# Half of batch 1's query turns by DMA, later loads of the query remainders, and one stored keys-by-values product for each batch, in a fused attention and expert layer

## The chip, the cores and the metric

One core of a Trainium2 chip. Times are device microseconds of that core, the median over runs in which the kernel before and the changed one alternate on the same chip. Profile times count from the start of the profiled span, which is some 1.8 us shorter than the timed run.

## The reference, cut to what matters

```python
def _attn_ref(q, k, v):                       # (8, 8, 576, 64) each
    q_s = softmax over the 64 channels of q   # cut: written out with max, exp, sum
    k_s = softmax over the 576 tokens of k
    kv  = einsum('bhsd,bhse->bhde', k_s, v)
    return einsum('bhsd,bhde->bhse', q_s, kv)

def _moe_ref(x, w_in, w_out, beta):           # x (4608, 512), d_ff = 2048
    h = x @ w_in
    return (h * sigmoid(beta * h)) @ w_out
```

Each batch's eight heads give 576 rows of x. The kernel treats 512 rows of each batch as a slab (slabs 0 to 7); the remaining 64 rows of all batches, the query remainders, form slab 8.

## The kernel before: the parts concerned

A slab has two passes on TensorE: pass 1 (x @ w_in, 64 matmuls of 128x512, ScalarE applies the activation), pass 2 (@ w_out, 64 more). The attention of the next batch is woven into pass 2 at given matmul counts. The queries must be turned (tokens to columns) for it: batch 1's on TensorE with a copy by ScalarE, later batches' by a transposing DMA. All loads go through SP's queue, in program order. Heads come in four pairs; QT holds turned queries, KVC the product of keys and values, XT the attention output in bf16.

```python
# batch 1's loads, in the stream that fills the first 45 us
load_wout(0); load_wout(4)
load_swapped(1, (0, 2, 3))      # query slots
load_wout(8)
load_swapped(1, (1,))
load_k(1, 4, (0, 1)); load_wout(12, 2); load_v(1, 4, (0, 1))
load_wout(14, 1); load_wout(15, 1)
for hp in (2, 3):
    load_k(1, 4, (hp,)); load_v(1, 4, (hp,))   # batch 1's last keys, last values

# slab 0, between its passes; then what is woven into pass 2 (counts from 65)
load(2)
scale_wout(0); scale_wout(4)                   # VectorE, w_out / beta
exp_q(1, (0, 1, 3, 2))                         # ScalarE
norm_main(1, 0, 1, POOL); norm_main(1, 1, 1, POOL); norm_main(1, 3, 1, POOL)
scale_wout(8)
norm_main(1, 2, 1, POOL)
todo = [(104, turn pairs 0, 1 on TensorE), (104.1, cast_v(1, 0) on ScalarE),
        (111, turn pairs 2, 3 on TensorE),
        (111.1, scale_wout(14, 2), exp_kc(1, 2), exp_kc(1, 3)),
        (116, kv_half(1, (7, 0), 0)),          # keys x values, pairs 0, 1
        (122, out_half(1, (1, 2), 0)), ...]    # outputs of pairs 0, 1 -> XT
# slab 1 starts
at(0, 0, 3)                                    # 3 matmuls of pass 1
kv_half(1, (7, 0), 2)                          # "second-half products": pairs 2, 3
at(1, 0, 3); at(0, 3, 5)
out_half(1, (7, 7, 7, 0), 2)                   # needs QT of pairs 2, 3
```

(The four lines of `todo` are paraphrased, the rest is cut.) The remainders of batches 0 to 3 are 16 small loads issued after batch 3's loads; the products of a remainder pair run in slabs 2, 3, 4 and 6.

The softmax here doesn't subtract the row's maximum and nothing guards it: scores larger than these inputs give would overflow.

Of the kernel before, what the change touches and what calls it, by code (L numbers as in the profile page):

```python
# [6 lines left out]
BF16 = mybir.dt.bfloat16  # L7
# [4 lines left out]
B = 8  # L12
# [151 lines left out]
def bass_efficient_attn_shen__then__act_swish_beta_kernel(  # L164
# [12 lines left out]
    with ExitStack() as es:  # L177
        def sb(name, shape, dt):
            return es.enter_context(nc.sbuf_tensor(name, shape, dt))
# [15 lines left out]
        VB = [sb(f"VB{i}", [128, NHP, NG, VW], BF16) for i in range(2)]  # L195
        QT = [sb(f"QT{i}", [128, NHP, SM], BF16) for i in range(2)]
        QTR = sb("QTR", [128, NHP, 128], BF16)
        KVC = [sb(f"KVC{i}", [128, NHP, D], BF16) for i in range(4)]
        RC = [sb(f"RC{i}", [128, NHP], F32) for i in range(2)]
        XT = [sb(f"XT{i}", [128, NM, SM], BF16) for i in range(2)]  # L200
        XT8 = sb("XT8", [128, NM, SM], BF16)
# [81 lines left out]
        def load(b):  # L283
            load_swapped(b)
            load_k(b)
            load_v(b)
            if b % 2:
                load_qrem(b - 1)


        for hp in range(NHP):
# [118 lines left out]
        def tile_mm(bk, ro, co, c, w, l, r_, start, stop, r):  # L410
            mm(PS[bk][co:co + 64, c:c + w], l, r_, start, stop, r=r, w=[("ps", bk)], bk=bk,
               tp=(ro, co))

        def kvc(b):
            return b + 2 if b < 2 else b % 2

        def quad(hp):
            return ((hp, 0, 0), (hp, 64, 64), (hp + 1, 0, 64), (hp + 1, 64, 0))
# [68 lines left out]
            out_evac(b, bks, (a, a + 1))  # L487

        def block(b):
            rem = {3: 3, 4: 1, 5: 5, 7: 7}.get(b)  # L490
            if b + 1 < B:
                kv_prods(b + 1, (1, 2), (0, 2))
            out_prods(b, (5, 6, 7, 0))
            if rem:
                outr_prods(rem, (1, 2))
            out_evac(b, (5, 6, 7, 0))
            if rem:
                outr_evac(rem, (1, 2))
            if b + 1 < B:
                kv_evac(b + 1, (1, 2))  # L500
# [16 lines left out]
        def kv_tiles(hp, bk):  # L517
            for j in range(NG):
                for c in (0, 64):
                    p = slice(c, c + 64)  # L520
                    tile_mm(bk, c, 64 - c if hp % 2 else c, 0, D + 1, EK[0][p, hp, j, :],
                            VB[0][p, hp, j, 0:D + 1], j == 0, j == NG - 1,
                            [("ekc", 0, hp), ("vb", 0, hp, 0), ("vb", 0, hp, 1), ("vone", 0)])
            add(DVE, lambda e: e.reciprocal(RC[0][:, hp:hp + 1], PS[bk][:, D:D + 1]),
                r=[("ps", bk)], w=[("rc", 0, hp)], bank=[bk])
            o, p_ = KVC[2][:, hp, :], PS[bk][:, 0:D]
            v_ = bass.AP(RC[0], hp, [[NHP, 128], [0, D]])
            add(DVE, lambda e: e.tensor_tensor(o, p_, v_, ALU.mult), r=[("ps", bk), ("rc", 0, hp)],
                w=[("kvc", 2, hp)], bank=[bk])

        def out_now(b, hp, bk, eng):
            i = b % 2
            for c in (0, 64):
                p = slice(c, c + 64)
                tile_mm(bk, c, 64 - c if hp % 2 else c, 0, SM, KVC[2][p, hp, :], QT[0][p, hp, :], True, True,
                        [("kvc", 2, hp), ("qt", 0, hp)])
            add(eng, lambda e: (e.copy if eng == ACTE else e.tensor_copy)(
                XT[i][:, hp, :], PS[bk][:, :]),
                r=[("ps", bk)], w=[("xt", i, hp)], bank=[bk])

        def go(steps):
            for s in steps:
                s()
# [143 lines left out]
                at(m)  # L687
        load_wout(0)
        load_wout(4)
        load_swapped(1, (0, 2, 3))  # L690
        load_wout(8)
        load_swapped(1, (1,))
        load_k(1, 4, (0, 1))
        load_wout(12, 2)
        load_v(1, 4, (0, 1))
# [51 lines left out]
        for t in range(NSLAB):  # L747
            todo = []
            if t == 0:
                def evacs():  # L750
                    o2_evac(0, 0, 3, DVE)
                    o2_evac(0, 1, 4, ACTE)

                todo = [(104, lambda: go(t_steps(1, (0, 1), (1,), ACTE))),
                        (104.1, lambda: cast_v(1, 0, ACTE)),
                        (111, lambda: go(t_steps(1, (2, 3), (2,), ACTE))),
                        (111.1, lambda: (scale_wout(14, 2), exp_kc(1, 2), exp_kc(1, 3))),
                        (116, lambda: kv_half(1, (7, 0), 0)),
                        (122, lambda: out_half(1, (1, 2), 0)), (124.5, evacs)]
            elif t == 1:  # L760
                todo = [(103, lambda: (kv_prods(2, (1, 2), (0, 2)), kv_evac(2, (1, 2)))),
                        (118, lambda: block(2))]
            elif t < 7:
                todo = [(104, lambda: block(t + 1))]
            todo = sorted(todo, key=lambda x: -x[0])
            slot = [0]

            def tick():
                slot[0] += 1
                while todo and todo[-1][0] <= slot[0]:  # L770
                    todo.pop()[1]()

            if 2 <= t < 7:
                if t < 5:
                    load(t + 2 if t == 2 else t + 3)
                for hp in (0, 2):
                    norm_main(t + 1, hp, 2)
                    t_dma(t + 1, hp, 2)
                if t in (2, 3, 4, 6):
                    norm_rem(t // 2 if t != 3 else 0)  # L780
                    tr_dma(t // 2 if t != 3 else 0)
                if t == 2:
                    load(5)
            elif t == 1:
                for hp in range(NHP):
                    cast_v(2, hp)
            if t < 2:
                slot[0] = NM * FIRST[t]
            for f in range(FIRST[t] if t < 2 else 0, NF):
                pass1_tile(t, f, tick)  # L790
            if t == 0:
                load(2)
                scale_wout(0)
                scale_wout(4)
                exp_q(1, (0, 1, 3, 2))
                norm_main(1, 0, 1, POOL)
                norm_main(1, 1, 1, POOL)
                norm_main(1, 3, 1, POOL)
                scale_wout(8)
                norm_main(1, 2, 1, POOL)  # L800
                exp_kc(1, 0, 2)
                scale_wout(12, 2)
                for hp in range(1, NHP):
                    cast_v(1, hp)
                pass2_group(0, (0, 1, 2, 3), (3, 4, 5, 6), tick)
                while todo:
                    todo.pop()[1]()
                at = by_m(1, 0, FIRST[1])
                o2_evac(0, 2, 5, ACTE)
                o2_evac(0, 3, 6, DVE)  # L810
                add(ACTE, lambda e: e.activation(DUMMY[:, 2:3], WARM[:, 0:1], ACT.Silu),
                    r=["warm"], w=["dummy"])
                at(0, 0, 3)
                kv_half(1, (7, 0), 2)
                at(1, 0, 3)
                at(0, 3, 5)
                out_half(1, (7, 7, 7, 0), 2)
                at(0, 5)
                at(1, 3)
                at(2)  # L820
                at(3)
                store(0)
                load(3)
                load_qrem(0)
                continue
            nb = [t + 2] if t + 2 < B else []
            if t == 1:
                nb = [2, 3]
            late = []
            for b in nb:  # L830
                if t == 1 and b == 2:
                    exp_q(2)
                    for hp in range(2):
                        norm_main(2, hp, 1, POOL)
                    t_dma(2, 0, 2)
                for hp in (0, 2):
                    exp_kc(b, hp, 2)
                if b > 2:
                    late.append(b)
                if b > 3:  # L840
                    for hp in range(NHP):
                        cast_v(b, hp)
            for b in late:
                exp_q(b)
                if b % 2 == 1:
                    exp_qr(b // 2)
                if b == 3:
                    exp_qr(0)
            for u in range(4):
                if (t, u) == (8, 3):  # L850
                    last_tile(u, ((0, 384), (384, 512)), (OB[orot[0] % 2], MB[0]))
                    continue
                pass2_group(t, (u,), (OB[orot[0] % 2],), tick)
                orot[0] += 1
                if t == 1 and u == 0:
                    for hp in range(2, 4):
                        norm_main(2, hp, 1, POOL if hp == 2 else DVE)
                    t_dma(2, 2, 2)
                    for hp in range(NHP):
                        cast_v(3, hp)  # L860
            while todo:
                todo.pop()[1]()
            if t < 8:
                store(t)
# [30 lines left out]
```

## Time and profile before

| | before |
|---|---|
| time, median of 3 (range) | 279.93 us (279.82 to 280.27) |
| span of the profile | 278.7 us |
| TensorE busy | 97% |
| stream of loads | 375 to 402 GB/s from 7 to 56 us |
| pass 2 of slab 0, first matmul to slab 1's first | 28.66 to 44.91 us |
| second-half products of batch 1 start | 45.68 us |

In a timeline line the columns are start, length, engine, source line, operation, output<-inputs, shapes, count; the bracket gives the idle time before the group and what ended it. PEld lines are TensorE's weight loads. In the trace of before, every change from 128x128 to 64x64 tiles shows 0.42 us of idle in the weight loads, whatever it is labelled, so only longer idle, or idle at another place, is read as a wait here. The prediction below shows the lines.

### The profile page before, as it was taken

The page shows a single profiled execution, that of the slowest core. Times are in us where ns is not written, and L with a number is a line of the kernel's source. Part 1 is how long each engine was busy: PE and PEld are TensorE (multiplying, and loading weights), DVE is VectorE, ACT ScalarE, POOL GpSimd, SP SyncE. Part 2 cuts the span into 40 slices and gives each one's busy share as a digit, 9 for nine tenths or more (in the row PEclk, how much of TensorE's full clock was granted, in tenths as well). Part 3 has the DMA queues.
Part 4 walks back from the last instruction along what each step waited for, and adds up shares of the span by engine and source line. Part 5 has one row for each costly group of instructions (what it writes and reads, how often), then busy time and mean ns, then how long its engine had stood idle before and what let it go on. Part 6 is the DMA issues. An engine that isn't in the chain of part 4 may idle for free.

```text
span 278.7 us, 4595 instructions
## 1 busy us (share of the span) xinstructions
PE 270.9 (97%) x1899; PEld 131.2 (47%) x1929; DVE 103.0 (37%) x204; ACT 166.5 (60%) x240; POOL 34.9 (13%) x52
## 2 busy tenths in 40 slices
PE   7999999999999999999999999999999999999995
PEld 3544444444445454545454544444444444444443
DVE  4744786008590149205730462035603300110012
ACT  4767667799577736793579437853751175027500
POOL 2630241207000304030002000000000000000000
PEclk9999999999999999999999999999999999999999
DMA  7999999996489799960599133002600120011022
GB/s 235 385 384 402 388 390 375 399 361 112 45 287 371 200 317 304 389 133 2 152 383 212 30 150 75 2 4 94 151 0 2 56 94 2 0 75 75 2 71 79
DMA packets 42173, 50.12 MB, mean 180 GB/s; under 512 B 21028, under 2 KB 29476, under 8 KB 41000
## 3 DMA queue, kind: packets, MB, share of 16 engines
q1 hardware_dynamic: 41312, 48.90, 55.3%
q10 hardware_dynamic: 840, 0.93, 1.0%
q8 instruction: 15, 0.25, 0.4%
q14 instruction: 6, 0.05, 0.0%
HBM read 36.71 MB, written 9.44 MB: 166 GB/s over the span
## 4 chain that ended last, share of the span: by engine, by line
PE 83%; DMA 11%; SPq 3%; issue 1%; DVE 0%
PE PS L372 83%; DMA O2S<-in_moe_w_out_dram 4%; DMA WST<-in_moe_w_out_dram 4%; DMA WST<-in_moe_w_in_dram 3%; SPq L250 1%; SPq L569 1%; SPq L293 0%; DVE WOUT L562 0%; SPq L298 0%; DVE WIN L573 0%; DVE O2S L724 0%; SPq L147 0%
## 5 line engine op out<-in xcount | busy, mean ns | idle before, releaser
L648 ACT ACTIVATE GT<-PS,BETA 128x512 bf16<-128x512 f32 x144 | 96.4, 690 | 61.9 <-PE PS L372 61.8
L372 PE MATMUL PS<-WOUT,GT 128*128 128x512 bf16 (+2 forms) x574 | 125.7, 373 | 2.0 <-issue 1.1
L372 PE MATMUL PS<-XT,WIN 128*128 128x512 bf16 x565 | 125.8, 379 | 0.9 <-issue 0.3
L372 PEld LDWEIGHTS PS<-XT,WIN 128*128 128x128 bf16 x576 | 60.2, 106 | 64.0 <-issue 1.0
L372 PEld LDWEIGHTS PS<-WOUT,GT 128*128 128x128 bf16 x592 | 56.4, 98 | 66.5 <-DVE WOUT L562 1.2
L703 DVE COPY O2S<-PS 128x512 f32<-128x512 f32 x33 | 22.7, 688 | 124.4 <-PE PS L372 124.3
L357 POOL CAST VB<-VF 128x576 bf16<-128x576 f32 x29 | 20.5, 707 | 85.4 <-DMA VF<-in_v_dram 84.2
L338 DVE TENSOR_REDUCE QS<-EQ 128x8 f32<-128x512 bf16 (+1 forms) x22 | 20.1, 913 | 17.6 <-ACT EQ L314 17.6
L459 ACT CAST XT<-PS 128x512 bf16<-128x512 f32 x14 | 7.6, 587 | 23.0 <-PE PS L372 22.8
L322 ACT ACTIVATE EK<-KF 128x1152 bf16<-128x1152 f32 (+1 forms) x19 | 18.4, 1005 | 4.1 <-DMA KF<-in_k_dram 3.9
L314 ACT ACTIVATE EQ<-QF 128x512 bf16<-128x512 f32 x32 | 17.7, 616 | 3.8 <-DMA QF<-in_q_dram 3.7
L340 DVE TENSOR_TENSOR EQ<-EQ,QI 128x1024 bf16<-128x1024 bf16 (+1 forms) x12 | 14.4, 1200 | 0.4
L340 POOL TENSOR_TENSOR EQ<-EQ,QI 128x512 bf16<-128x512 bf16 x10 | 10.5, 1048 | 31.5 <-DVE QI L339 31.2
L459 DVE CAST XT<-PS 128x512 bf16<-128x512 f32 x14 | 9.1, 687 | 12.7 <-PE PS L372 12.7
L372 PEld LDWEIGHTS PS<-VB,EK 64*64 64x64 bf16 x576 | 6.6, 107 | 4.5 <-issue 2.5
L372 PE MATMUL PS<-VB,EK 64*64 64x65 bf16 x576 | 7.9, 193 | 0.4 <-POOL VB L357 0.3
L372 PE MATMUL PS<-XT 128*128 128x512 f32 x6 | 5.3, 1050 | 1.5 <-DVE XT L226 1.5
L648 ACT ACT_TABLE_LOAD x5 | 6.4, 1283 | 0.1
L372 PE MATMUL PS<-QT,KVC 64*64 64x512 bf16 x64 | 6.2, 383 | 0.1
L562 DVE TENSOR_SCALAR WOUT<-O2S,RB 128x512 bf16<-128x512 f32 x8 | 5.2, 686 | 1.0 <-DMA O2S<-in_moe_w_out_dram 0.9
L339 DVE RECIPROCAL QI<-QS 128x8 f32<-128x8 f32 (+1 forms) x22 | 5.0, 226 | 0.8
L322 ACT ACT_TABLE_LOAD x4 | 5.1, 1283 | 0.1
(51 smaller groups left out, 68.0 us busy)
## 6 DMA issues: line engine op xcount, KB each, us to landing
out_dram<-O2S SPq DMA_DIRECT2D x8, 1024.0 KB, 4.6
QF<-in_q_dram SPq DMA_DIRECT2D x30, 256.0 KB, 6.1
KF<-in_k_dram SPq DMA_DIRECT2D x6, 1152.0 KB, 8.6
VF<-in_v_dram SPq DMA_DIRECT2D x6, 1152.0 KB, 11.8
KF<-in_k_dram SPq DMA_DIRECT2D x8, 288.0 KB, 8.4
VF<-in_v_dram SPq DMA_DIRECT2D x8, 288.0 KB, 8.8
WST<-in_moe_w_in_dram SPq DMA_DIRECT2D x8, 256.0 KB, 7.3
O2S<-in_moe_w_in_dram SPq DMA_DIRECT2D x4, 512.0 KB, 11.7
```

Source lines behind the costliest of these rows:

```text
L250: add(engs[c % len(engs)], lambda e, a=a, o=o: e.dma_start(o, a), w=[(name, i, hp) for hp in range(c * n, c * n + n)], slot=f"{name}{i}_{c}")
L314: add(ACTE, lambda e, o=o, a=a: e.activation(o, a, ACT.Exp), r=[("qf", i, hp, x) for x in ((2, 3) if hp % 2 else (hp // 2,))], w=[("eq", i ...
L322: add(ACTE, lambda e: e.activation(o, a, ACT.Exp), r=[("kf", i, h) for h in range(hp, hp + n)], w=[("ekc", i, h) for h in range(hp, hp + n)])
L338: add(DVE, lambda e: e.tensor_reduce(s_, a, AX.X, ALU.add), r=ks, w=[("qs", i, hp0)])
L339: add(DVE, lambda e: e.reciprocal(v_, s_), r=[("qs", i, hp0)], w=[("qi", i, hp0)])
L340: add(eng, lambda e: e.tensor_tensor(a, a, vb, ALU.mult), r=ks + [("qi", i, hp0)], w=ks)
L357: add(eng, lambda e: (e.copy if eng == ACTE else e.tensor_copy)(o, a), r=[("vf", i, hp), ("vone", i)], w=[("vb", i, hp, h) for h in ((0, 1 ...
L372: add(PE, lambda e: e.matmul(o, l, r_, start=start, stop=stop, tile_position=tp), r=r, w=w, bank=[bk])
L459: add(eng, lambda e, eng=eng, bk=bk, hp=hp: (e.copy if eng == ACTE else e.tensor_copy)(XT[i][:, hp, :], PS[bk][:, :]), r=[("ps", bk)], w=[ ...
L562: add(DVE, lambda e, f=f: e.tensor_scalar(WOUT[:, f, :], STAGE[f // 4][:, f % 4, :], RB[:, f:f + 1], None, ALU.mult), r=[SKEY[f // 4][f % ...
L648: add(ACTE, lambda e: e.activation(GT[:, f, :], PS[bk][:, :], ACT.Silu, scale=BETA[:, f:f + 1]), r=[("ps", bk), "beta"], w=[("gt", f)], ba ...
L703: add(eng, lambda e: (e.copy if eng == ACTE else e.tensor_copy)(O2S[t % 2][:, u, :], PS[bk][:, :]), r=[("ps", bk)], w=[("o2", t % 2, u)], ...
```

## The change

Its intent is to take eight turns off TensorE, to bring output weights 8 to 11 sooner, and to move the 16 remainder loads out of the way of batch 2's turns.

The diff is shortened: lines are joined and the dots and words in `todo` stand for code.

```diff
-        KVC = [... for i in range(4)]
+        KVC = [... for i in range(B)]
-            if b % 2: load_qrem(b - 1)                  # in load(b)
-            rem = {3: 3, 4: 1, 5: 5, 7: 7}.get(b)
+            rem = {4: 3, 5: 1, 6: 5, 7: 7}.get(b)
-        load_swapped(1, (0, 2, 3)); load_wout(8); load_swapped(1, (1,))
+        load_swapped(1, (0, 2)); load_wout(8); load_swapped(1, (3, 1))
-                todo = [(104, turn pairs 0, 1), ..., (111, turn pairs 2, 3), ...
+                todo = [(107, turn pairs 0, 1), ...                  # no second turn
-                load(2)
                 scale_wout(0); scale_wout(4); exp_q(1, (0, 1, 3, 2))
                 norm_main(1, 0, 1, POOL)
+                scale_wout(8)
                 norm_main(1, 1, 1, POOL); norm_main(1, 3, 1, POOL)
-                scale_wout(8)
-                norm_main(1, 2, 1, POOL)
                 exp_kc(1, 0, 2); scale_wout(12, 2)
+                norm_main(1, 2, 1)                      # on VectorE
+                t_dma(1, 2, 2)
+                load(2)
-                load_qrem(0)                            # after load(3) in slab 0
+                    load_qrem(2); load_qrem(0)          # after batch 2's turns, slab 1
```

Cut: later remainders behind the turns of slabs 3 and 4, their exponentials and turns a slab later, some counts in `todo` moved by two or three matmuls, and the exponentials of the last keys moved from count 111 to 119.

More of the change, by code (lines that the diff above doesn't have):

```diff
@@ L197, in bass_efficient_attn_shen__then__act_swish_beta_kernel @@
         QTR = sb("QTR", [128, NHP, 128], BF16)
-        KVC = [sb(f"KVC{i}", [128, NHP, D], BF16) for i in range(4)]
+        KVC = [sb(f"KVC{i}", [128, NHP, D], BF16) for i in range(B)]
         RC = [sb(f"RC{i}", [128, NHP], F32) for i in range(2)]
@@ L286, in load @@
             load_v(b)
-            if b % 2:
-                load_qrem(b - 1)
         for hp in range(NHP):
@@ L414, in kvc @@
         def kvc(b):
-            return b + 2 if b < 2 else b % 2
+            return b
         def quad(hp):
@@ L525, in kv_tiles @@
                 r=[("ps", bk)], w=[("rc", 0, hp)], bank=[bk])
-            o, p_ = KVC[2][:, hp, :], PS[bk][:, 0:D]
+            o, p_ = KVC[0][:, hp, :], PS[bk][:, 0:D]
             v_ = bass.AP(RC[0], hp, [[NHP, 128], [0, D]])
             add(DVE, lambda e: e.tensor_tensor(o, p_, v_, ALU.mult), r=[("ps", bk), ("rc", 0, hp)],
-                w=[("kvc", 2, hp)], bank=[bk])
+                w=[("kvc", 0, hp)], bank=[bk])
         def out_now(b, hp, bk, eng):
@@ L534, in out_now @@
                 p = slice(c, c + 64)
-                tile_mm(bk, c, 64 - c if hp % 2 else c, 0, SM, KVC[2][p, hp, :], QT[0][p, hp, :], True, True,
-                        [("kvc", 2, hp), ("qt", 0, hp)])
+                tile_mm(bk, c, 64 - c if hp % 2 else c, 0, SM, KVC[0][p, hp, :], QT[0][p, hp, :], True, True,
+                        [("kvc", 0, hp), ("qt", 0, hp)])
             add(eng, lambda e: (e.copy if eng == ACTE else e.tensor_copy)(
@@ L689, in bass_efficient_attn_shen__then__act_swish_beta_kernel @@
         load_wout(4)
-        load_swapped(1, (0, 2, 3))
+        load_swapped(1, (0, 2))
         load_wout(8)
-        load_swapped(1, (1,))
+        load_swapped(1, (3, 1))
         load_k(1, 4, (0, 1))
@@ L752, in evacs @@
                     o2_evac(0, 1, 4, ACTE)
-                todo = [(104, lambda: go(t_steps(1, (0, 1), (1,), ACTE))),
-                        (104.1, lambda: cast_v(1, 0, ACTE)),
-                        (111, lambda: go(t_steps(1, (2, 3), (2,), ACTE))),
-                        (111.1, lambda: (scale_wout(14, 2), exp_kc(1, 2), exp_kc(1, 3))),
-                        (116, lambda: kv_half(1, (7, 0), 0)),
-                        (122, lambda: out_half(1, (1, 2), 0)), (124.5, evacs)]
+                todo = [(107, lambda: go(t_steps(1, (0, 1), (1,), ACTE))),
+                        (107.1, lambda: cast_v(1, 0, ACTE)),
+                        (111.1, lambda: scale_wout(14, 2)), (119.1, lambda: (exp_kc(1, 2), exp_kc(1, 3))),
+                        (118, lambda: kv_half(1, (7, 0), 0)),
+                        (124, lambda: out_half(1, (1, 2), 0)), (124.5, evacs)]
             elif t == 1:
@@ L778, in bass_efficient_attn_shen__then__act_swish_beta_kernel @@
                     t_dma(t + 1, hp, 2)
-                if t in (2, 3, 4, 6):
-                    norm_rem(t // 2 if t != 3 else 0)
-                    tr_dma(t // 2 if t != 3 else 0)
+                if t > 2:
+                    pi = (1, 0, 2, 3)[t - 3]
+                    norm_rem(pi)
+                    tr_dma(pi)
+                if t == 3:
+                    load_qrem(4)
+                if t == 4:
+                    load_qrem(6)
                 if t == 2:
@@ L844, in bass_efficient_attn_shen__then__act_swish_beta_kernel @@
                 exp_q(b)
-                if b % 2 == 1:
-                    exp_qr(b // 2)
-                if b == 3:
-                    exp_qr(0)
+                for pi in {4: (1, 0), 6: (2,), 7: (3,)}.get(b, ()):
+                    exp_qr(pi)
             for u in range(4):
@@ L858, in bass_efficient_attn_shen__then__act_swish_beta_kernel @@
                     t_dma(2, 2, 2)
+                    load_qrem(2)
+                    load_qrem(0)
                     for hp in range(NHP):
```

## The prediction

> **What bounds the kernel now.** The page comes first: TensorE is busy for 97% of the span, and the chain that ended last is 83% TensorE with the rest in front of it.
>
> ```profile
> span 278.7 us, 4595 instructions
> PE 270.9 (97%) x1899; PEld 131.2 (47%) x1929; DVE 103.0 (37%) x204; ACT 166.5 (60%) x240; POOL 34.9 (13%) x52
> ```
>
> Busy is not working, so I asked the waits of TensorE by stretch. From 80 us to the end there are five gaps of 0.16 us, all labelled issue, each after a block of 64x64 products. The steady stretches run 49 matmuls in 10.74 us, 0.219 us each, with the granted clock at 1.00. After 48 us nothing that this change touches stands in front of TensorE, unless the change puts it there. So the second view is the chain in order of time, for the first 48 us:
>
> ```profile
> 10.28 9.53 DMA WST<-in_moe_w_in_dram
> 19.83 0.44 DVE WIN L573
> ...
> 20.33 9.86 DMA WST<-in_moe_w_out_dram
> 30.19 11.39 DMA O2S<-in_moe_w_out_dram
> ...
> 41.61 0.50 DVE WOUT L562
> 42.10 4.06 PE PS L372 x53
> ```
>
> Up to 42 us the end is set by the one stream of loads: the page's slices show 375 to 402 GB/s from 7 to 56 us. Third, the timeline of TensorE, of its weight loads and of the helpers around the second pass of slab 0 (28.7 to 44.9 us), into which batch 1's attention is woven:
>
> ```profile
> 37.87 0.61 PE L370 MATMUL PS<-IDB,EQ 128*128 128x128 bf16 x8
> 38.32 1.67 PE L372 MATMUL PS<-WOUT,GT 128*128 128x512 bf16 x7
> 39.83 0.61 PE L370 MATMUL PS<-IDB,EQ 128*128 128x128 bf16 x8
> 40.27 1.24 PE L372 MATMUL PS<-WOUT,GT 128*128 128x512 bf16 x5
> ```
> ```profile
> 35.81 0.55 PEld L372 LDWEIGHTS PS<-WOUT,GT 128*128 128x128 bf16 x4 [0.57 <-DVE WOUT L562]
> 36.99 0.11 PEld L372 LDWEIGHTS PS<-WOUT,GT 128*128 128x128 bf16 x2 [0.64 <-DVE WOUT L562]
> 45.14 0.12 PEld L372 LDWEIGHTS PS<-XT,WIN 128*128 128x128 bf16 x2 [0.35 <-ACT XT L459]
> ```
> ```profile
> 43.94 0.68 ACT L322 ACTIVATE EK<-KF 128x576 bf16<-128x576 f32 x1 [0.89 <-DMA KF<-in_k_dram]
> 44.52 0.57 ACT L459 CAST XT<-PS 128x512 bf16<-128x512 f32 x1
> ```
>
> The reader is to see three things. Each group of eight turns takes 0.44 us of TensorE (37.87 to 38.32, 39.83 to 40.27). The output weights 8 to 11 came late: 39 matmuls took 28.66 to 37.87, 9.21 us, where 39 x 0.219 = 8.55 were due, so 0.66 us was lost. And after the pass TensorE waits for ScalarE's copy of pair 1 into XT, which ended at 45.09 because ScalarE stood before it on batch 1's last keys, landed at 43.94. That last gate decides: what is saved ahead of it is handed back there.
>
> **What the Trainium skill says.** "TensorE: Matmul & The Clock Gate", Part 4: PE-mode transpose, says a turn on TensorE goes to PSUM and needs a copy afterwards, and gives about 275 ns in a kernel. The trace agrees on the copy (ScalarE, 1.0 us for two pairs); one turn's mean is 220 ns, but eight in a row cost only 0.44 us, and that is what I use. "Advanced Engine Details and Errata", X-Bar Transpose (TRN2), calls transposing transfers as fast as regular ones, at 350 to 400 GB/s. The trace disagrees: a turn of two pairs (256 KB) takes 3.1 us from issue to landing with idle queues, and its packets move some 210 GB/s. "DMA: Bandwidth & Descriptors", Queues, rings and completion order, says that SP has one ring on each of the 16 DMA engines, consumed in ring order. The trace agrees: the turn issued at 81.67 landed 10.8 us later at 92.5, about 1.1 us after the values ahead of it (GpSimd started casting them at 91.50). "SBUF — State Buffer", SBUF: two separate sides, says that GpSimd and VectorE share one port pair under an exclusive lock; here scaling one output weight took a mean 0.48 us out of WST, nearly all with GpSimd idle, and 0.69 out of O2S, mostly beside GpSimd's multiplies.
>
> **The change part by part.**
>
> *Turns of pairs 2 and 3.* It removes 8 turns (0.44 us of TensorE) and one copy of 1.0 us on ScalarE, which had slack. It adds one transposing transfer and moves the multiply of pair 2 from GpSimd to VectorE (0.69 to 0.98 us).
>
> *Order of loads.* Query slot 3 (256 KB) goes behind output weights 8 to 11. At about 390 GB/s that is 0.67 us: issued 23.33, landed 11.9 us later at 35.2, they should now land at 34.55. VectorE scales them at once, since the sums of pairs 1 and 3 now follow them: 34.55 to about 36.3. TensorE needs weight 8 at 28.66 + 32 x 0.219 = 35.67, so the 0.66 us is gone.
>
> *VectorE after that.* Sums of pairs 1 and 3, four instructions, 36.3 to 38.0. Weights 12 and 13 (landed 38.7) to about 40.0 to 40.4. All of pair 2: 0.68 + 0.20 + 0.69 to 0.98 = 1.6 to 1.9 us, to about 41.7 to 42.2. Then weights 14 and 15 until 42.6 to 43.1; before they were done at 42.10. Then batch 1's first KVC, 0.76 us, at 43.4 to 43.9.
>
> *TensorE with it.* 43 matmuls from 28.66 end at 38.08; 8 turns to 38.6; 11 matmuls to 41.06; products of keys and values to 41.6; two matmuls to 42.1. Weight 14 is ready at about 42.2 to 42.6: wait 0.1 to 0.5. Weights 15 similar, to 43.3; first output products after KVC, at 43.5 to 44.0; four last matmuls, so the pass ends at 44.9 to 45.3, where it ended at 44.9 before. XT of pair 1 still follows the keys landed at 43.94, so it is there at 45.1 to 45.2. Then 0.44 us of matmuls, products of the second half at about 45.7, as before (45.68). Sum: 0.66 + 0.44 = 1.1 us saved, then about 1.1 us of waiting, net 0 to +0.3.
>
> *The transfer.* Its source is ready at about 42; batch 1's values, ahead in the ring, land at 44.73, so about 1.1 us later, 45.8, with 42 + 5.1 = 47.1 (the slowest lightly loaded landing) as the bad case. TensorE needs it at 47.3. Hidden, narrowly.
>
> *Query remainders.* The same 16 issues leave 54 to 67 us (13.1 us on SP) and follow batch 2's turns, at about 68.8. Uncongested they cost about 0.64 + 0.04 us each, 10.9 in all, to 79.7; the store of slab 1 and batch 4's loads thus start 3.0 us late (before, 76.71). Batch 4's values landed at about 91.4, now 94.4; GpSimd's four casts (2.86 us) end at 97.4 and their products stand at 98.3. Hidden with 1 us to spare. The remainder products only move by a slab, 16 each time, 0.3 us; TensorE's total is unchanged. Keeping KVC for all batches costs memory and no time.
>
> **The rivals.** *One: the gate moves too.* Before, batch 2's loads ran behind batch 1's; from 42 to 43 us most packets were already theirs, 1 KB each:
>
> ```profile
> DMA packets 341, 0.36 MB, mean 364 GB/s; under 512 B 24, under 2 KB 310, under 8 KB 341
> ```
>
> So only few DMA engines still held batch 1. If the later start of batch 2's loads lets these hurry, keys and values land earlier and some of the 1.1 us stays: up to 0.3 us if the rest of 2.7 us runs a tenth faster, 279.6. Against it: the last four landed 0.75 us apart, as one engine at its own pace would. *Two: the transfer is late* and TensorE stands at its output products: 0.3 to 1 us more, 280.2 to 280.9. For it: the margin of 0.2 in the bad case. Against it: the ring is nearly drained by then. *Three: the remainders push batch 4* past 98.3: up to 1 us, about 280.7. For it: a congested issue took 0.8 us, 2 to 3 us more over 16. *Four: the whole saving survives*, 278.8; against it stand the keys that land no sooner.
>
> **Range and chances.** 279.93 with net 0 to +0.3 from the sum, a chance of -0.3 from rival one and a quarter's chance of +0.5 from two or three: 279.8 to 280.0; I say 279.9. Range 279.2 to 280.9. Two per cent is 5.6 us; no term above reaches it: 0.97 for same.
>
> **What would show it.** No idle before weights 8 to 11 in TensorE's weight loads near 36 us; one group of turns, not two, before 45 us; a wait for WOUT or KVC at 42 to 44 us; the second half's products near 45.7; no wait on QT near 47; batch 4's casts near 94.5, ended by 98. The prediction is wrong if the second half's products start well before 45.4, if TensorE waits for QT or VB in slabs 0 to 2, or if batch 1's keys land much before 43.9.

## The result, and the profile after

| | before | changed |
|---|---|---|
| median of 4 runs on one chip (range) | 280.10 us (279.82 to 280.73) | 279.88 us (279.72 to 280.30) |
| ratio changed / before | | 0.9991, 95% interval 0.9970 to 1.0013 |
| span of the profile | 278.7 us | 278.2 us |

The time is the same. First the chain of the changed kernel's profile that ended last, in order of time:

```profile
33.05 10.25 DMA KF<-in_k_dram
...
43.32 0.68 ACT EK L320
44.00 0.48 ACT XT L457
...
44.53 5.67 PE PS L370 x60
```

Before, the last transfer on the chain was output weight 15. Now it is batch 1's last keys: their exponentials (ScalarE), then ScalarE's copy of pair 1 into XT, then TensorE without a break. That is the gate the prediction named. Next the changed kernel's TensorE and its weight loads, in this order:

```profile
28.24 9.44 PE L370 MATMUL PS<-WOUT,GT 128*128 128x512 bf16 x43
37.52 0.75 PE L368 MATMUL PS<-IDB,EQ 128*128 128x128 bf16 x8
38.10 2.64 PE L370 MATMUL PS<-WOUT,GT 128*128 128x512 bf16 x11
...
43.90 0.38 PE L370 MATMUL PS<-XT,WIN 128*128 128x512 bf16 x1
44.53 0.61 PE L370 MATMUL PS<-XT,WIN 128*128 128x512 bf16 x2 [0.26 <-ACT XT L457]
45.07 0.48 PE L370 MATMUL PS<-VB,EK 64*64 64x65 bf16 x36
```
```profile
41.62 0.11 PEld L370 LDWEIGHTS PS<-WOUT,GT 128*128 128x128 bf16 x2 [0.43 <-DVE WOUT L560]
42.02 0.15 PEld L370 LDWEIGHTS PS<-WOUT,GT 128*128 128x128 bf16 x2 [0.28 <-DVE WOUT L560]
...
44.53 0.12 PEld L370 LDWEIGHTS PS<-XT,WIN 128*128 128x128 bf16 x2 [0.65 <-ACT XT L457]
```

One group of turns is left, and the 43 matmuls before it start 0.216 us apart ((37.52 - 28.24) / 43): nothing waits for weights 8 to 11 any more. From pass 2's first matmul to slab 1's first, TensorE takes 15.66 us (28.24 to 43.90) in place of 16.25. But the loads of weights 14 and 15 into TensorE wait for VectorE, and the second matmul of slab 1 waits for XT.

One pair of traces is not enough for this length, since it scatters. Kernels with the old work of pass 2 took 15.92 to 16.25 us (before, k_rem, b_gate below); those with the changed work and the same loads took 15.22 to 15.69 (the changed kernel, a_again, a_gate, a_best, a_rem24). So TensorE did save time in pass 2, about 0.5 us in the mean. In a_again, which is the changed kernel once more, no weight load of pass 2 waits for WOUT: it took 15.22 us, and all the waiting is at XT.

The profiled run began pass 2 0.42 us sooner than the one of before (28.24 against 28.66), and so did everything after it. That is no effect of the change: run k_rem below, whose work up to there is that of before, began pass 2 at 28.34.

### The profile page after: what moved, and what is told of

The parts are those of the page before. It is cut to its first block, busy times and chain, and to the rows that moved or that the text cites. A ratio compares the mean times of both kernels' runs of the same rounds, so it can differ in the third digit from the quotient of the medians.

```text
span 278.2 us, 4609 instructions
## 1 busy us (share of the span) xinstructions
PE 273.0 (98%) x1921; PEld 130.7 (47%) x1921; DVE 101.7 (37%) x205; ACT 165.4 (59%) x239; POOL 33.9 (12%) x51
## 4 chain that ended last, share of the span: by engine, by line
PE 83%; DMA 11%; SPq 3%; DVE 1%; ACT 0%; issue 0%
PE PS L370 83%; DMA KF<-in_k_dram 4%; DMA WST<-in_moe_w_out_dram 4%; DMA WST<-in_moe_w_in_dram 3%; SPq L250 2%; SPq L567 1%; DVE WOUT L560 1%; SPq L291 0%; ACT EK L320 0%; ACT XT L457 0%; SPq L296 0%; DVE WIN L571 0%; SPq L556 0%; DVE O2S L722 0%; SPq L147 0%
## 5 line engine op out<-in xcount | busy, mean ns | idle before, releaser
L370 PE MATMUL PS<-WOUT,GT 128*128 128x512 bf16 (+2 forms) x592 | 127.8, 373 | 0.0
L338 POOL TENSOR_TENSOR EQ<-EQ,QI 128x512 bf16<-128x512 bf16 x9 | 9.4, 1042 | 27.6 <-DVE QI L337 27.2
L370 PE MATMUL PS<-XT 128*128 128x512 f32 x6 | 4.5, 900 | 1.5 <-DVE XT L226 1.5
L560 DVE TENSOR_SCALAR WOUT<-O2S,RB 128x512 bf16<-128x512 f32 x8 | 3.8, 526 | 2.6 <-DMA O2S<-in_moe_w_out_dram 2.6
```

The costliest lines, as they stand in the source:

```text
L338: add(eng, lambda e: e.tensor_tensor(a, a, vb, ALU.mult), r=ks + [("qi", i, hp0)], w=ks)
L370: add(PE, lambda e: e.matmul(o, l, r_, start=start, stop=stop, tile_position=tp), r=r, w=w, bank=[bk])
L560: add(DVE, lambda e, f=f: e.tensor_scalar(WOUT[:, f, :], STAGE[f // 4][:, f % 4, :], RB[:, f:f + 1], None, ALU.mult), r=[SKEY[f // 4][f % ...
```

## The experiments

Twelve kernels ran, each timed in five rounds beside the kernel before. The theory to be tested: about 1.1 us is saved on TensorE, and a gate (the landing of batch 1's last keys, plus ScalarE's work on them) takes it back. Rivals: the gate itself moved; nothing was saved; a later wait took it.

**The three parts, each alone on the kernel before.**

```diff
# k_order
-        load_swapped(1, (0, 2, 3)); load_wout(8); load_swapped(1, (1,))
+        load_swapped(1, (0, 2)); load_wout(8); load_swapped(1, (3, 1))
+        scale_wout(8) ahead of the sums of pairs 1 and 3; first turn at 107
```

> The kernel before with only the order of loads and of VectorE's work changed (query slot 3 behind output weights 8 to 11, weights scaled before the sums of pairs 1 and 3, turns three matmuls later). Theory: TensorE's 0.66 us of waiting for weights 8 to 11 goes, and comes back as waiting for WOUT, KVC or XT before the second-half products: time within 0.2 us of before. Rival (the waits near 36 us were what held the kernel): -0.6 us.

Measured: 280.57 us, ratio 1.0013 (0.9997 to 1.0029): same. The weights came in time, and TensorE then stood where the second group of turns needs pair 2, whose sums VectorE now does later. TensorE's timeline of this run:

```profile
37.72 1.03 PE L372 MATMUL PS<-WOUT,GT 128*128 128x512 bf16 x4
39.40 0.62 PE L370 MATMUL PS<-IDB,EQ 128*128 128x128 bf16 x8 [0.66 <-POOL EQ L340]
```

The wait near 36 us went, and 0.66 us of idle came near 39 us, at a place that the expectation did not name: pass 2 took 16.50 us, against 15.92 to 16.25 for the old order. The new order takes the wait away only where pairs 2 and 3 are not turned on TensorE.

```diff
# k_turn
-                load(2)                                  # ahead of scale_wout(0)
                 norm_main(1, 2, 1, POOL)
+                t_dma(1, 2, 2)
+                load(2)
-                (111, turn pairs 2, 3 on TensorE)
```

> The kernel before with only pairs 2 and 3 of batch 1 turned by DMA, and batch 2's loads behind that. Theory: 0.44 us of TensorE goes and comes back at the gate; the transfer lands about 1 us after batch 1's last values and before it is needed: within 0.2 us of before. Rival one (batch 2's later loads let batch 1's last keys land sooner): from the landing of batch 1's third keys to that of its last values 2.1 us in place of 2.36, and up to -0.3 us. Rival two (the transfer is late): TensorE waits for QT, +0.3 us or more.

Measured: 280.59 us, ratio 1.0018 (0.9997 to 1.0039): same by the interval, with a wait that the trace shows. The transfer for batch 1 was not late; the one for batch 2, a slab later, was. TensorE's timeline of this run:

```profile
72.33 0.41 PE L372 MATMUL PS<-QT,KVC 64*64 64x512 bf16 x4
73.57 0.41 PE L372 MATMUL PS<-QT,KVC 64*64 64x512 bf16 x4 [0.82 <-DMA QT<-EQ]
```

SP had issued the 16 remainder loads from 55.66 to 67.73 us and came to batch 2's turns only then. Of the expectation's first rival half is there: from the third keys to the last values it was 2.24 us, where 2.1 was set for the rival and 2.36 for before.

```diff
# k_rem: KVC for all batches and every edit of the remainders, nothing else
```

> The kernel before with only the query remainders moved and KVC kept for all batches. Theory: batch 4's values land 3 to 4 us later, their casts end within 0.5 us of the start of the second half of their products, so nothing or 0.1 us is lost: within 0.2 us of before. Rival (batch 4's products wait): +0.5 to +1 us, and a wait for VB near 98 us.

Measured: 279.83 us, ratio 0.9989 (0.9976 to 1.0002): same. This kernel saves nothing on TensorE in pass 2, and yet its ratio is that of the changed kernel (0.9991 and 0.9989): another sign that the saving does not reach the end. Batch 4's values landed at 95.23 us in place of 91.50. Then turn and remainders together (k_turn plus k_rem):

> The kernel before with the turn by DMA and with the remainders moved, the order of loads left as it was. In the run with the turn alone TensorE stood 0.82 us for QT in slab 1, because the 16 remainder loads stood ahead of batch 2's turns and batch 2's loads started later. Theory: with the remainders behind those turns this wait is gone, and nothing else is gained, because batch 1's keys still hold slab 1: within 0.2 us of before, about 0.4 us under the run with the turn alone. Rival (the late turn came from batch 2's later loads, not from the remainders): the wait for QT near 73 us stays, +0.3 to +0.8 us over before.

Measured: 279.83 us, ratio 0.9992 (0.9978 to 1.0006): same. No wait for QT is left in its trace. So the remainders' move pays for the turn: without it the turn costs 0.8 us in slab 1. The rival (batch 2's later loads) is out, since these are just as late here.

**Where the saving goes.** The strongest reading needs no edit. In every trace that waits at the gate, the distance from the keys' landing (the start of ScalarE's exponentials that a DMA released) to the second-half products is the same:

| kernel | last keys at | second-half products | distance | last pass of slab 8 starts | distance from the keys |
|---|---|---|---|---|---|
| before | 43.94 | 45.68 | 1.74 | 261.74 | 217.80 |
| changed | 43.32 | 45.07 | 1.75 | 261.26 | 217.94 |
| changed, again (a_again) | 42.95 | 44.70 | 1.75 | 260.77 | 217.82 |
| k_rem | 43.21 | 45.01 | 1.80 | 261.19 | 217.98 |
| k_turn_rem | 43.27 | 45.02 | 1.75 | 261.12 | 217.85 |
| k_turn | 43.04 | 44.79 | 1.75 | 262.02 | 218.98 |

With or without the change the kernel ends a nearly fixed time after these keys land; k_turn alone adds its 0.82 us for QT. In before and k_rem TensorE comes to the gate just as it opens (0.77 and 0.74 us from slab 1's first matmul to the products, against 0.74 with the gate moved away in b_gate below); in the changed kernel it comes early and stands there. (In a_rem24, below, the distance to the products is 1.74 us; in k_order, b_less and a_less, where TensorE comes after the gate has opened, it is longer.) The keys land anywhere from 42.95 to 43.94 us, which is scatter of the runs: before and k_rem do the same work up to there and differ by 0.73 us. Two lines of ScalarE, in the second run of the changed kernel, give the 1.75 us: the exponentials, the copy (which ends at 44.11), and then 0.6 us on TensorE until the products start at 44.70.

```profile
42.95 0.68 ACT L320 ACTIVATE EK<-KF 128x576 bf16<-128x576 f32 x1 [0.70 <-DMA KF<-in_k_dram]
43.54 0.57 ACT L457 CAST XT<-PS 128x512 bf16<-128x512 f32 x1
```

> The changed kernel unchanged, timed once more beside these runs. Both theories: 0 to -0.3 us against before; second-half products 1.75 us after batch 1's last keys land, as in the five traces so far that show a wait at the gate.

Measured: 279.56 us, ratio 0.9989 (0.9977 to 1.0002): same, and 1.75 us as expected.

**Opening the gate by an order of ScalarE.**

```diff
# a_gate (on the changed kernel); b_gate is the same on the kernel before
-  (119.1, lambda: (exp_kc(1, 2), exp_kc(1, 3)))
+  (119.1, lambda: exp_kc(1, 2))
-  (124, lambda: out_half(1, (1, 2), 0))
+  (124, lambda: (out_half(1, (1, 2), 0), exp_kc(1, 3)))
```

> The changed kernel, with ScalarE copying pair 1 into XT before it takes the exponentials of batch 1's last keys (right result). Theory: the idle of 0.65 us in the weight loads before the second matmul of slab 1 goes; the next thing to wait for are the last values, cast 0.7 us after they land, so the second-half products start 0.2 to 0.3 us sooner and the time falls by 0.1 to 0.3 us. Rival (the key gate is not what holds TensorE): no change, within 0.1 us in the trace.

> The kernel before with only the gate opened (ScalarE copies pair 1 into XT before the exponentials of batch 1's last keys). Theory: TensorE of the kernel before comes to the gate only 0.1 us ahead of its opening, so 0 to -0.2 us; less than the -0.48 us that the same edit gave on the changed kernel. Rival (that edit is worth 0.5 us by itself, whatever was saved before it): -0.4 to -0.5 us.

Measured: a_gate 279.36 us, ratio 0.9983 (0.9967 to 0.9999); b_gate 280.13 us, ratio 1.0004 (0.9991 to 1.0016). TensorE around slab 1's first matmul, in a_gate, then before, then b_gate:

```profile
44.13 0.88 PE L370 MATMUL PS<-XT,WIN 128*128 128x512 bf16 x3
44.94 0.57 PE L370 MATMUL PS<-VB,EK 64*64 64x65 bf16 x36
```
```profile
44.91 0.85 PE L372 MATMUL PS<-XT,WIN 128*128 128x512 bf16 x3
45.68 0.48 PE L372 MATMUL PS<-VB,EK 64*64 64x65 bf16 x36
```
```profile
44.23 0.81 PE L372 MATMUL PS<-XT,WIN 128*128 128x512 bf16 x3
44.97 0.55 PE L372 MATMUL PS<-VB,EK 64*64 64x65 bf16 x36
```

From slab 1's first matmul to the second-half products, the changed kernel took 1.17 us (43.90 to 45.07) and 1.14 in its second run, a_gate 0.81 (44.13 to 44.94). The kernel before took 0.77 (44.91 to 45.68) and b_gate 0.74 (44.23 to 44.97). So the edit takes away 0.35 us of waiting on the changed kernel and 0.03 on the kernel before, as the theory has it: only the changed kernel arrives early. That this reaches the end is not shown: the two times agree in sign, but their intervals overlap. (The 0.48 us in b_gate's expectation is a_gate against the kernel before. Against the changed kernel's second run a_gate is 0.2 us lower, on another chip.) From pass 2's start to the products a_gate took 16.41 us, the changed kernel 16.83 in its first trace and 16.36 in its second, in which the stream was early (batch 1's last values landed 15.35 us after that start, against 15.79 in a_gate and 15.81 in the first trace).

**Opening the gate from the side of the stream.** Output weights 14 and 15 are not loaded (a wrong result), so that the keys land sooner.

```diff
# b_less (kernel before), a_less (changed kernel)
-        load_wout(14, 1)
-        load_wout(15, 1)
```

> The kernel before, without the loads of output weights 14 and 15 (512 KB less ahead of batch 1's last keys; the result is wrong on purpose, the stage holds old numbers). Theory (savings ahead of the gate are handed back at the gate, which is batch 1's keys landing): the keys land about 1.3 us sooner, but the kernel before reaches the gate only when it opens, so almost nothing follows: -0.1 us against before (0 to -0.3). Rival (the kernel before is already held by the stream of loads there): about -1 us.

> The changed kernel, with the same two loads left out (wrong on purpose). Theory: here TensorE stands 0.5 us at the gate, so the gate's earlier opening is worth 0.4 to 0.7 us: second-half products start 0.5 us sooner after the start of slab 0's second pass than in the changed kernel (16.8 us after it, now about 16.3), and the time is 0.4 to 0.7 us under before. Rival (the change saves nothing on TensorE, no wait at the gate): same as the kernel before without the two loads, within 0.2 us.

Measured: b_less 279.93 us, ratio 1.0007 (0.9989 to 1.0024); a_less 279.81 us, ratio 0.9997 (0.9981 to 1.0013). For the kernel before the keys came by 42.05 us and nothing was gained, as expected (16.89 us from pass 2's start to the products, where before, k_rem and b_gate have 16.66 to 17.02). For the changed kernel the expectation missed: the keys came by 42.23 us, the wait at XT went, and yet the products started 16.79 us after pass 2's start, against 16.83. The trace of a_less shows what stepped in, in the weight loads:

```profile
41.76 0.11 PEld L370 LDWEIGHTS PS<-WOUT,GT 128*128 128x128 bf16 x2 [0.42 <-DVE WOUT L560]
42.56 0.11 PEld L370 LDWEIGHTS PS<-WOUT,GT 128*128 128x128 bf16 x2 [0.69 <-DVE WOUT L560]
```

VectorE scaled weights 14 and 15 in 1.28 us (from 41.23) in place of 0.88, while GpSimd cast values (from 41.54) that in the changed kernel landed only at 42.68; that the cast slowed it is not tested by itself. So the keys are not the only gate: just ahead of them stands VectorE's work on pair 2 and on the last weights.

**Opening all of them.**

```diff
# a_open = a_gate and
-                norm_main(1, 2, 1)
+                norm_main(1, 2, 1, POOL)
-                at(0, 0, 3); kv_half(1, (7, 0), 2); at(1, 0, 3)
+                at(0, 0, 3); at(1, 0, 3); kv_half(1, (7, 0), 2)
# a_best = a_gate, the second edit of a_open, and load_qrem(0) moved from slab 1 to slab 2
```

> The changed kernel with all three gates opened: the copy before the last keys' exponentials, pair 2's multiply back on GpSimd so that VectorE scales weights 14 and 15 at once, and three more matmuls of slab 1 ahead of the second-half products (right result). Theory: the 1.1 us saved on TensorE reaches the end, less what the landing of weight 15 still costs: 0.5 to 1.0 us under the kernel before, no idle over 0.5 us on WOUT, XT or VB in the weight loads between 38 and 48 us. Rival (the saving was not there, or a further gate follows): within 0.2 us of before.

> The changed kernel with the gate opened, three more matmuls of slab 1 ahead of the second-half products, and the second pair's remainders loaded in slab 2 rather than ahead of batch 4 (right result). Theory: the last 0.2 us of waiting before the second-half products and the 0.1 us on batch 4's values go: 0.5 to 0.8 us under before, and no wait for VB in slab 2. Rival (VectorE's weights 14 and 15 and the transfer of pairs 2 and 3 take their place): no better than the changed kernel with the gate opened, -0.3 to -0.5 us.

Measured: a_open 281.32 us, ratio 1.0052 (1.0035 to 1.0069): 0.5% slower, clear of the noise though under the 2% that counts here, and its expectation missed. It was a mistake of the experiment, and a telling one: GpSimd multiplies pair 2 ahead of its cast of pair 1's values, and TensorE waits for that cast:

```profile
40.30 0.22 PE L370 MATMUL PS<-VB,EK 64*64 64x65 bf16 x2
42.04 0.47 PE L370 MATMUL PS<-VB,EK 64*64 64x65 bf16 x34 [1.53 <-POOL VB L355]
```

a_best: 279.97 us, ratio 1.0001 (0.9989 to 1.0014), no gain; its expectation missed. The wait for VB in slab 2 is gone (batch 4's values land at 91.49), but the weight loads still show 1.1 us of idle on WOUT in three places at the end of slab 0, as in a_gate, and 0.63 us on XT in slab 1 (at 48.40 us), where a_gate has 0.20. Its rival, waits that take each other's place, held in kind; its size, -0.3 to -0.5 us, did not. I found no version that beats both kernels clearly: a_gate has the lowest median, 0.2 us under a_again's on another chip, which these intervals don't separate.

**The price of the remainders.** Eight more of the small loads at the same place:

```diff
# a_rem24 (on the changed kernel)
                     load_qrem(2); load_qrem(0)
+                    load_qrem(2)
```

> The changed kernel with the eight loads of one pair's query remainders issued once more at the same place (24 in place of 16; right result). Theory (the time that SP takes to issue them pushes everything behind it, and the margin of batch 4 is used up): 8 x 0.77 = 6.2 us more of issuing, batch 4's values land 6 us later and TensorE waits for VB in slab 2: 5 to 6.5 us more than the changed kernel. Rival (the issues are hidden as before, there is room): 0 to 1 us more.

Measured: 286.77 us, ratio 1.0241 (1.0222 to 1.0261), 6.9 us over the changed kernel's 279.88 and more than the 5 to 6.5 expected, though the issues took only 5.5 us longer (17.78 against 12.30). SP's queue, first in the changed kernel, then here:

```profile
68.22 12.30 SPq L261 DMA_DIRECT2D QRF<-in_q_dram  x16
80.58 0.59 SPq L707 DMA_DIRECT2D out_dram<-O2S  x1
```
```profile
68.00 17.78 SPq L261 DMA_DIRECT2D QRF<-in_q_dram  x24
85.83 0.60 SPq L707 DMA_DIRECT2D out_dram<-O2S  x1
```

Then TensorE of this run in slab 2, and its engines in the stretch from 95 to 108 us (busy time and count for each engine, granted clock, DMA share, GB/s):

```profile
101.16 0.26 PE L370 MATMUL PS<-VB,EK 64*64 64x65 bf16 x2 [3.67 <-POOL VB L355]
101.89 0.99 PE L370 MATMUL PS<-VB,EK 64*64 64x65 bf16 x36 [0.47 <-POOL VB L355]
103.35 0.70 PE L370 MATMUL PS<-VB,EK 64*64 64x65 bf16 x34 [0.47 <-POOL VB L355]
```
```profile
95.00:108.00 13.00, 8.36 (x103) 3.69 (x102) 2.99 (x8) 7.69 (x11) 2.67 (x4) 0.74 1.05 323
```

The store and batch 4's loads behind the remainders moved by 5.3 us, and 4.6 us of it reached TensorE as waits: the margin for batch 4 was indeed used up. The remaining 2 us or so are the clock, 0.74 in this stretch where the changed kernel has 1.00. In shorter windows it is 0.50 from 100.0 to 106.8 us; TensorE worked for some 4.7 us of that, which at half the clock costs an estimated 2.3 us. The Trainium skill, "TensorE: Matmul & The Clock Gate", Part 1: The HAM clock gate, says that the clock falls to half after an idle window of about 3.4 us. This run agrees on the half; but the fall came about 2.5 us after TensorE's last matmul (97.5 us by the trace), sooner than the page's window, within a gap of 3.67 us.

## Why the prediction was right

- *The stretch that decides.* Right. From the second-half products to the last pass of slab 8 it is 216.19 us against 216.06 before, and 216.07 in the second run, and the chain ran through batch 1's last keys.
- *Weights 8 to 11 in time.* Right: scaled from 34.12 us (34.54 with this run's earlier start of 0.42 us added, forecast 34.55), and no wait. What that was worth is 0.57 us in this trace of before, not 0.66: the turns are woven in at count 104, counted from 65, so 40 matmuls stand ahead of them (one record is missing in the trace), and they are due 0.216 us apart. In the six traces with the old order it was 0.16 to 0.57 us.
- *What TensorE saves.* Right in sum within the scatter, too large in its first term, distributed otherwise. With the 0.57 the saving is about 1.0 us, and less against the other runs with the old order. I had expected pass 2 to give nearly all of it back by waiting for weights 14 and 15 and KVC; it kept 0.59 us (16.25 to 15.66), and 1.03 in the second run, and then the gate took 0.4 us (1.17 and 1.14 against 0.77). From pass 2's start to the second-half products it is 16.83 and 16.36 us in the changed kernel, 17.02 in before and 16.67 in k_rem: about 0.25 us less in the mean, where I had forecast 0 to 0.3 more, and within the scatter. So that the time came out within 0.1 us of 279.9 is partly luck.
- *The signs of being wrong.* The products start at 45.07 us (45.49 with the 0.42 added), against "well before 45.4". The second run has 44.70, but k_rem, with the old work, has 45.01, so that sign was narrower than the scatter. No wait for QT or VB in slabs 0 to 2 goes beyond the 0.42 us of a change of tiles.
- *The transfer for pairs 2 and 3.* Right: issued at 41.24, landed 3.8 us later at 45.0 (forecast 45.8), needed at 46.67, no wait.
- *The remainders.* The mechanism was right, the size off: 12.30 us for 16 issues, 0.77 each, where I took 0.68 and 10.9. Batch 4's values landed at 95.17, not 94.4, the casts ended at 98.03, and the promised margin of 1 us was nothing: those products began at 97.64, before the casts had ended, and took 0.92 us in place of 0.83.
- *Rival one, the gate moves too.* Partly there. From the landing of pair 2's keys to that of the last values it is 2.36, 2.32 and 2.29 us where batch 2's loads follow at once (before, k_rem, b_gate), 2.24 in the two with the later loads alone (k_turn, k_turn_rem), and 2.09 to 2.15 in five of six traces that have the changed order and the later loads (2.29 in a_open; a_less, with loads left out, is not counted). That is up to about 0.2 us, below what the times resolve.
- *What I did not see.* That the parts lean on each other: the order alone moves the wait to the turns (k_order), the turn alone makes batch 2's turn late (k_turn); only the remainders' move stands alone (k_rem).

What stays open: how much of the median's 0.2 us is real. Both measurements of the changed kernel have ratios just under one (0.9991, 0.9989) and intervals that hold one. And no run took VectorE's gate away with success (a_open was to), so its share is read from the waits in the traces and from a_less.

## What to carry to other kernels

Before removing work from a busy engine, look for the next transfer that it will have to wait for: the distance from a landing to the engine's next step, compared over several runs, tells whether the end follows the engine or the transfer. Work saved ahead of such a gate gave nothing clear of the noise here, and opening one by reordering a helper engine can close another (a_open lost 1.4 us that way). The small loads on SP's queue were priced by their issue time, 0.74 to 0.77 us each, and whatever stood behind them in that queue paid it.

## What the Trainium skill lacked or had wrong

- "Advanced Engine Details and Errata", X-Bar Transpose (TRN2): transposing transfers "as fast as regular DMAs". Here a turn of 256 KB took 3.1 us with idle queues, its packets moving some 210 GB/s, where plain loads ran at 375 to 402 GB/s. The section's figure does not hold for these turns.
- "DMA: Bandwidth & Descriptors", Issuing engines are not separate DMA queues: the time on the sequencer to start a transfer is "usually small relative to the DMA itself". For 16 remainder loads of 32 KB in a row it is not: 0.77 us each to issue (12.30 us in all), while 32 KB at the stream's 390 GB/s would be an estimated 0.08 us. (One such load still takes longer to land than to issue: 3.3 us for the last of the 16 in before.)
- No page that I found gives a time for the change between 128x128 and 64x64 tiles. In the trace of before the weight loads are idle for 0.42 us at each change from 128x128 to 64x64 tiles, and TensorE for up to 0.16 us after such blocks (the changed kernel's first trace shows no such idle after 48 us, its second does), which can be mistaken for a wait.
- "TensorE: Matmul & The Clock Gate", Part 1: The HAM clock gate: the idle window of about 3.4 us. In a_rem24 the clock fell about 2.5 us after TensorE's last matmul (one case).
